# The first two units' inverses: from one pass over 32 rows through DRAM to 16-row blocks joined on TensorE

## The chip, the cores and the metric

The kernel runs on one core of a Trainium2 chip. The metric is the device time of one execution in microseconds (us); lower is better. TensorE is called PE here, VectorE DVE, ScalarE ACT, GpSimd POOL, and SyncE, whose queue issues most DMAs, SP.

## What is computed

A delta-rule attention over 768 tokens for 4 batches of 8 heads of width 48, then an MLP with a squared ReLU on the joined heads. Inputs are float32 (q, k, v, beta) and float64 (the MLP's weights).

```python
k_n = k / (norm(k) + 1e-6)
for t in range(S):                       # S = 768
    y[:, :, t] = q[:, :, t] @ state
    v_old = k_n[:, :, t] @ state
    state = state + beta[:, :, t] * outer(k_n[:, :, t], v[:, :, t] - v_old)
x = y, the 8 heads side by side          # 3072 tokens x 384
out = max(x @ w_in, 0) ** 2 @ w_out      # w_in 384 x 2048, w_out 2048 x 384
```

## The kernel before

**Units.** The work is cut into 12 units of 128 tokens of two batches (6 stretches of time, two pairs of batches). Within a unit the recurrence over a chunk of 64 tokens is put as matrix products: for each chunk and head, the inverse T of a unit triangular 64 x 64 matrix made of k k^T and beta. With T, a chunk's values and keys are transformed (`whole`, L439), and the state is carried through the two chunks (`sequential`, L488). The two pairs of batches have a state each, so units 0 and 1 both start from an empty state and do not depend on each other.

**The inverse.** `static` (L296) transposes k and q on PE, copies them to `kq` with ACT and multiplies k by k and k by q. The diagonal 32 x 32 blocks of k k^T go through DRAM (`blocks`), so that each of up to 128 partitions holds one block (`lt`). `invert` (L386) inverts all blocks on DVE by 31 steps of a product (L413, or L415 with beta as a scalar) and a subtraction (L416). The result goes through DRAM again (`inv`) into `tt` and `t1t`, and `whole` puts the off-diagonal 32 x 32 block together with two small products on PE (L454, L462), a copy (L456) and a negation (L466). For units 0 and 1 one call of `invert` treats both units' blocks, one block a partition, 31 steps of up to 256 elements.

**The MLP.** `moe` (L534) transposes y (L541), splits it in a high and a low half of a reduced float32 format (x_h, x_l), and multiplies it with the weights' high and low halves: nine matmuls a tile of 128 hidden columns (L574), then relu, square and cast on ACT (L581, L582, L584), the low half on DVE (L553) and the products with w_out (L561), for 16 hidden tiles taken two by two.

**The weights.** 28 pieces (12 of w_in, 512 columns wide; 16 of w_out, 384 wide) come as float64 (`fetch`, L122) and are turned into a high and a low half (`split_weights`, L135), in place: the halves take the raw piece's room. For a piece: `least` (L138) takes the absolute value of the upper word on ACT (L142) and clamps it from below on POOL (L143); `words` (L146) is four DVE operations (L150, L153, L156, L157), the last of which reads the lower word; `high` (L161) is a cast on ACT (L163); `low` (L166) adds the rest up in PSUM with two or three matmuls (L170, L171) and copies the low half out with ACT (L172). In the first period the remainder a - high is formed on DVE (`remainder`, L177). `least` is issued three pieces ahead in the beginning and one ahead in the first period.

**Order.** PE, DVE, ACT and SP work through their instructions in the order in which the Python code emits them; generators yield between steps, and the order is written by hand. The prologue (L665 to L710) loads, normalises, forms the products of units 0 and 1, inverts both, and carries unit 0 through its state part, with 18 pieces of the weights taken between. Then come eleven periods (L714). Period u interleaves by fractions of the period (`weave`, L613) the MLP of unit u-1, the state part of unit u, the products of unit u+1, its inversion, and the loads and normalisation of unit u+2; in period 1 also the other 10 pieces of the weights. PE's work is the same in every later period.

Weights are fetched by SP in the order of use: three pieces after the loads of k, three and more between the loads of q, the rest (`fetch(NW)`, L698) ahead of the inversion.

Of the kernel before, what the change touches and what calls it, by code (L numbers as in the profile page):

```python
# [20 lines left out]
def kernel(  # L21
# [74 lines left out]
    ttile = []  # L96
    for i in range(2):
        tt = const.tile([P, NC, H, C], F32, name=f"tt{i}")
        nc.gpsimd.memset(tt[:, :, :, :HB], 0.0)
        ttile.append(tt)  # L100
# [19 lines left out]
    AHEAD = 20  # L120
# [10 lines left out]
    def room(x, n):  # L131
        pool, first, second = rooms[x % 2 if x < AHEAD - 1 else 0]
        return pool.tile([P, PC], I32, name=first)[:, :n], pool.tile([P, PC], I32, name=second)[:, :n]

    def split_weights():  # L135


        def least(x):  # L138

            w1 = raws[x][:, :, 1]  # L140
            a, rest = room(x, w1.shape[1])
            nc.scalar.activation(out=a.bitcast(F32), in_=w1.bitcast(F32), func=AF.Abs)  # L142
            nc.gpsimd.tensor_scalar(out=a.bitcast(F32), in0=a.bitcast(F32), scalar1=LEAST, scalar2=None, op0=ALU.max)  # L143
            return x, a, rest

        def words(x, a, rest):  # L146
            raw = raws[x]
            w1 = raw[:, :, 1]

            nc.vector.tensor_scalar(out=a, in0=a, scalar1=3, scalar2=0x3FFFFFF8,  # L150
# [15 lines left out]
        def low(x, a, rest, hl, formed=False):  # L166
            ps = split_bank()[:, :hl.shape[2]]
            first = [(plus, hl[:, 1])] if formed else [(ident, a.bitcast(F32)), (minus, hl[:, 0])]
            for m, y in first:
                nc.tensor.matmul(ps, lhsT=m, rhs=y, start=(m is first[0][0]), stop=False)  # L170
# [4 lines left out]
        def remainder(x, a, rest, hl):  # L175

            nc.vector.tensor_tensor(out=hl[:, 1], in0=a.bitcast(F32), in1=hl[:, 0].bitcast(F32), op=ALU.subtract)  # L177

        before, ready, x = None, [], 0
        while split_early:  # L180

            far = 3 if x < AHEAD - 3 else 1
            while len(ready) < far:
                ready.append(least(x + len(ready)))
            if x == 0:
                yield
            now = high(*words(*ready.pop(0)))
            if before:
                low(*before)
            before = now  # L190
            x += 1
            while len(ready) < (far if x < AHEAD - 3 else 1):
                ready.append(least(x + len(ready)))
            yield
# [571 lines left out]
```

## Time and profile before

| | |
|---|---|
| median of 3 runs | 695.78 us (695.34 to 696.73) |
| profiled execution: span, first to last instruction | 691.8 us; its own time is not given apart from it, the three runs lie 3.5 to 4.9 us above it |
| PE busy | 628.9 us, 91% of the span |
| DVE busy | 433.1 us, 63% |
| ACT busy | 332.8 us, 48% |
| POOL busy | 76.4 us, 11% |
| mean granted PE clock | 0.966 |
| a later period (transposes of unit 2's MLP at 217.0, of unit 1's at 168.4) | 48.6 us |

The page shows busy times by engine, the span in 40 slices (about 17.3 us each, busy tenths as digits), and groups of instructions: line, engine, operation, written tile <- read tiles, shape, count | busy us, mean ns | idle time of the engine ahead of them and what ended it. A timeline row has the start and the length in us; DMA rows have the time that issuing took.

### The profile page before, as it was taken

The page shows a single profiled execution, that of the slowest core. Times are in us where ns is not written, and L with a number is a line of the kernel's source. Part 1 is how long each engine was busy: PE and PEld are TensorE (multiplying, and loading weights), DVE is VectorE, ACT ScalarE, POOL GpSimd, SP SyncE. Part 2 cuts the span into 40 slices and gives each one's busy share as a digit, 9 for nine tenths or more (in the row PEclk, how much of TensorE's full clock was granted, in tenths as well). Part 3 has the DMA queues.
Part 4 walks back from the last instruction along what each step waited for, and adds up shares of the span by engine and source line. Part 5 has one row for each costly group of instructions (what it writes and reads, how often), then busy time and mean ns, then how long its engine had stood idle before and what let it go on. Part 6 is the DMA issues. An engine that isn't in the chain of part 4 may idle for free.

```text
span 691.8 us, 23593 instructions
## 1 busy us (share of the span) xinstructions
PE 628.9 (91%) x10084; PEld 583.2 (84%) x10084; DVE 433.1 (63%) x1175; ACT 332.8 (48%) x632; POOL 76.4 (11%) x94
## 2 busy tenths in 40 slices
PE   1740797889999999999999999999999999999997
PEld 0530366779999999999999999999999999999997
DVE  3789776898468387477485494694674775641221
ACT  3630455763453544544535535535545445354352
POOL 8540332310100100001001001001000010000000
PEclk9985689999999999999999999999999999999999
DMA  7678620410441531532423414405315324030100
GB/s 158 158 207 290 195 48 5 91 24 2 89 81 20 103 67 23 107 55 39 96 48 55 99 28 77 90 17 114 65 18 107 58 36 97 3 61 3 24 2 23
DMA packets 174712, 49.95 MB, mean 72 GB/s; under 512 B 166400, under 2 KB 169488, under 8 KB 174608
## 3 DMA queue, kind: packets, MB, share of 16 engines
q1 hardware_dynamic: 172016, 47.85, 32.4%
q8 instruction: 79, 1.29, 0.8%
q10 hardware_dynamic: 2336, 0.59, 0.4%
q14 instruction: 25, 0.20, 0.1%
q0 software_dynamic: 256, 0.01, 0.1%
HBM read 37.32 MB, written 11.01 MB: 70 GB/s over the span
## 4 chain that ended last, share of the span: by engine, by line
PE 78%; DVE 4%; ACT 1%; issue 1%; DVEq 0%
PE h L574 30%; PE o L561 29%; PE g L505 3%; PE g L481 3%; PE x L518 2%; PE x L474 2%; PE x L327 2%; PE g L526 1%; PE g L327 1%; PE g L317 1%; PE x L317 1%; PE h L541 1%; PE x L462 1%; PE x L454 1%; DVE tmp L415 1%
## 5 line engine op out<-in xcount | busy, mean ns | idle before, releaser
L561 PE MATMUL o<-w,h_h 128*128 128x384 f32 x768 | 203.7, 346 | 0.0
L574 PE MATMUL h<-x_h,w 128*128 128x256 f32 x1152 | 173.4, 286 | 1.7 <-ACT x_h L543 1.7
L574 PEld LDWEIGHTS h<-x_h,w 128*128 128x128 f32 x1152 | 153.6, 189 | 7.3 <-ACT x_h L543 2.0
L553 DVE TENSOR_TENSOR h_l<-r,h_h 128x512 fp32r<-128x512 f32 x96 | 66.6, 694 | 147.9 <-PE o L561 61.5
L581 ACT ACTIVATE r<-h 128x512 f32<-128x512 f32 x96 | 57.5, 599 | 179.0 <-PE h L574 178.7
L561 PEld LDWEIGHTS o<-w,h_h 128*128 128x128 f32 x768 | 133.2, 188 | 2.4
L561 PE MATMUL o<-w,h_l 128*128 128x384 f32 x384 | 129.8, 338 | 0.0
L415 DVE SCALAR_TENSOR_TENSOR tmp<-lt,bt,z 128x126 f32<-128x126 f32 (+22 forms) x310 | 95.4, 308 | 22.7 <-DMA out_dram<-a 10.5
L574 PE MATMUL h<-x_l,w 128*128 128x256 f32 x576 | 99.8, 282 | 0.0
L416 DVE TENSOR_TENSOR z<-z,tmp 128x126 f32<-128x126 f32 (+22 forms) x310 | 79.2, 255 | 10.7
L574 PEld LDWEIGHTS h<-x_l,w 128*128 128x128 f32 x576 | 82.1, 190 | 0.0
L561 PEld LDWEIGHTS o<-w,h_l 128*128 128x128 f32 x384 | 72.2, 188 | 0.0
L582 ACT ACTIVATE r<-r 128x512 f32<-128x512 f32 x96 | 60.7, 632 | 3.0
L584 ACT CAST h_h<-r 128x512 fp32r<-128x512 f32 x96 | 59.5, 620 | 3.1
L399 POOL MEMSET z<- 128x512 f32 x10 | 5.3, 532 | 401.4 <-DMA inv<-z 355.0
L143 POOL TENSOR_SCALAR a<-a 128x384 f32<-128x384 f32 (+1 forms) x19 | 26.6, 1399 | 47.0 <-ACT a L142 46.8
L274 DVE TENSOR_REDUCE n<-rest 128x8 f32<-128x384 f32 x20 | 10.8, 549 | 31.5 <-ACT rest L273 31.5
L466 ACT ACTIVATE tt<-x 32x256 f32<-32x256 f32 x42 | 15.7, 375 | 26.3 <-PE x L462 25.8
L170 PE MATMUL o<-r,plus 128*128 128x512 f32 (+1 forms) x16 | 10.4, 737 | 19.8 <-DVE r L153 19.8
L543 ACT CAST x_h<-h 128x384 fp32r<-128x384 f32 x24 | 11.6, 482 | 32.2 <-PE h L541 32.2
L505 PEld LDWEIGHTS g<-state,kq 48*64 48x64 f32 x1408 | 22.5, 134 | 4.3 <-issue 2.8
L481 PE MATMUL g<-vt,tt 64*64 64x48 f32 x768 | 25.8, 223 | 0.0
(143 smaller groups left out, 774.2 us busy)
## 6 DMA issues: line engine op xcount, KB each, us to landing
w<-in_moe_w_in_dram SPq DMA_DIRECT2D x12, 512.0 KB
w<-in_moe_w_out_dram SPq DMA_DIRECT2D x16, 384.0 KB
lt<-blocks SPq DMA_DIRECT2D x22, 256.0 KB
vt<-in_v_dram SPq DMA_DIRECT2D x96, 48.0 KB
out_dram<-a SPq DMA_DIRECT2D x46, 96.0 KB
kpad<-in_k_dram SPq DMA_DIRECT2D x88, 48.0 KB
qpad<-in_q_dram SPq DMA_DIRECT2D x88, 48.0 KB
blocks<-ap SPq DMA_DIRECT2D x48, 64.0 KB
```

Of the source, the lines that this page charges most:

```text
L143: nc.gpsimd.tensor_scalar(out=a.bitcast(F32), in0=a.bitcast(F32), scalar1=LEAST, scalar2=None, op0=ALU.max)
L327: nc.tensor.matmul(ps[j][b * C:(b + 1) * C, p], lhsT=kq[rows, c, p, b, 0], rhs=kq[rows, c, p, b, first:first + n].rearrange("p x t -> p (x ...
L415: nc.vector.scalar_tensor_tensor(out=tmp, scalar=bt[:, s:s + 1], op0=ALU.mult, op1=ALU.mult, **factors)
L416: nc.vector.tensor_tensor(out=z[:, :nj, s + 1:], in0=z[:, :nj, s + 1:], in1=tmp, op=ALU.subtract)
L481: nc.tensor.matmul(g[rows, c, h], lhsT=tt[rows, c, h], rhs=vt[rows, c, h], start=True, stop=True)
L505: nc.tensor.matmul(dst[to * C:(to + 1) * C, j, p], lhsT=kq[rows, c, p, b, x], rhs=s[rows, b, p], start=(x == 0 and p == 0), stop=False, sk ...
L553: nc.vector.tensor_tensor(out=h_l, in0=r, in1=h_h.bitcast(F32), op=ALU.subtract)
L561: nc.tensor.matmul(o[i], lhsT=a[:, e, i * P:(i + 1) * P], rhs=halves["wo", ft][w], start=(ft == 0 and n == 0), stop=(ft == FT - 1 and n == 2))
L574: nc.tensor.matmul(hp[:, e], lhsT=halves["wi", (kt, ft // EACH)][w][:, f], rhs=x[:, kt], start=(n == 0), stop=(n == 3 * KT - 1))
L581: nc.scalar.activation(out=r, in_=hp, func=AF.Relu)
L582: nc.scalar.activation(out=r, in_=r, func=AF.Square)
L584: nc.scalar.copy(out=h_h, in_=r)
```

## The change

It touches the prologue, the first period and the weights' conversion. The rest of the periods is as before.

- **Inverses of units 0 and 1.** A new generator `first_pair` takes both units together. It multiplies k by k in 32 x 32 blocks directly on PE, diagonal and off-diagonal ones; turns the diagonal blocks with DVE transposes so that each partition holds rows of 16 x 16 blocks; inverts those on DVE in 15 steps; and joins 16-row blocks to 32 and 32-row blocks to 64 with small matmuls. Nothing of it goes through DRAM. beta comes in 32 small DMAs from POOL's queue in place of 16. Its large temporaries use rooms of weights that are fetched later.
- **State parts.** `whole` is split: what follows the inverse is `applied`. Units 0 and 1 both go through `applied` and `sequential` in the prologue, and the two transposes of unit 0's MLP too; period 1 has no state part.
- **Normalisation.** One call takes k of units 0 and 1 together.
- **Weights.** The clamp moves from POOL to DVE. Absolute value, clamp, the four word operations and the cast stand together in one step, with nothing issued ahead; the low half is always formed by three matmuls. A step of the generator is now a high half or a low half. 22 steps (12 high halves, 10 low ones) are taken in the prologue and 34 in period 1. Pieces 0 to 9 alternate between two pairs of rooms (before 0 to 18).
- **Loads.** k of both units comes ahead of all weights; q, v and 15 weights follow; the loads of unit 2 come next, and the last 13 weights behind them.

The core of the diff; the parts of `first_pair` that shape its blocks are shortened.

```diff
-    AHEAD = 20
+    AHEAD = 10
...
-        def least(x):
-            w1 = raws[x][:, :, 1]
-            a, rest = room(x, w1.shape[1])
-            nc.scalar.activation(out=a.bitcast(F32), in_=w1.bitcast(F32), func=AF.Abs)
-            nc.gpsimd.tensor_scalar(out=a.bitcast(F32), in0=a.bitcast(F32), scalar1=LEAST, scalar2=None, op0=ALU.max)
-            return x, a, rest
-        def words(x, a, rest):
+        def words(x):
             raw = raws[x]
             w1 = raw[:, :, 1]
+            a, rest = room(x, w1.shape[1])
+            nc.scalar.activation(out=a.bitcast(F32), in_=w1.bitcast(F32), func=AF.Abs)
+            nc.vector.tensor_scalar(out=a.bitcast(F32), in0=a.bitcast(F32), scalar1=LEAST, scalar2=None, op0=ALU.max)
...
+        before = None
+        for x in range(NW):
+            now = high(*words(x))
+            yield
             if before:
                 low(*before)
+                yield
             before = now
...
+    def first_pair(ds):
...
+        for r in range(2):
+            for j in range(2):
+                for half in range(2):
+                    for i, d in enumerate(ds):
...
+                        for e in range(2):
+                            nc.gpsimd.dma_start(out=bt[at + e:at + HS:2, j], in_=src[:, :, e * HS:(e + 1) * HS])
...
+        near = blocks(0)
+        yield
+        f = apool.tile([P, 2, HS, 2, HS], F32, name="lt", bufs=1)
+        gs = wide(NW - 7, 2, 2 * NX, HB)
+        for j in range(2):
+            nc.scalar.copy(out=gs[:, j], in_=near[j])
+            nc.vector.transpose(out=f[:, j].rearrange("p t e s -> p (t e s)"),
+                                in_=gs[:, j].rearrange("p i (e t) -> p t (i e)", e=2))
+        yield
+        os = wide(NW - 6, 2, 2 * NX, HB)
+        for j, ps in enumerate(blocks(1)):
+            nc.scalar.copy(out=os[:, j], in_=ps)
+        yield
...
+        for s in range(HS - 1):
+            nj, nt = s + 1, HS - 1 - s
+            tmp = room[:, :2 * nj * nt].rearrange("p (x j t) -> p x j t", x=2, j=nj)
+            nc.vector.tensor_tensor(out=tmp, in0=lt[:, :, s:s + 1, s + 1:].broadcast_to([P, 2, nj, nt]),
+                                    in1=z[:, :, :nj, s:s + 1].broadcast_to([P, 2, nj, nt]), op=ALU.mult)
+            nc.vector.tensor_tensor(out=z[:, :, :nj, s + 1:], in0=z[:, :, :nj, s + 1:], in1=tmp, op=ALU.subtract)
...
+        nc.vector.tensor_tensor(out=all_heads(slice(HS, HB)), in0=all_heads(slice(HS, HB)), in1=ps, op=ALU.subtract)
+        t1 = apool.tile([P, 2 * H2, HB], F32, name="lt", bufs=1)
+        nc.vector.transpose(out=t1, in_=all_heads(slice(0, HB)))
+        nc.scalar.copy(out=all_heads(slice(HB, C)), in_=all_heads(slice(0, HB)))
...
-    NS = 3 * (NW + 1 - (1 + 6 + 4 + 7)) + 2
+    NS = 2 * NW - 22
...
+        ds_.append(load(1))
+        pair = first_pair(ds_[:])
+        take(pair, 1)
+        fetch(3)
         load_q(ds_[0])
         fetch(2)
         load_q(ds_[1])
+        fetch(4)
+        for d in ds_:
+            load_v(d)
+        fetch(6)
+        take(normalize(*ds_))
+        take(pair, 1)
         take(splits, 1)
+        take(pair, 1)
+        take(splits, 1)
+        take(splits, 1)
+        take(splits, 1)
+        take(pair, 2)
+        take(splits, 1)
+        take(pair, 1)
+        take(splits, 1)
+        take(pair, 1)
         ds_.append(load(2))
         load_q(ds_[2])
         load_beta(ds_[2])
+        take(pair, 1)
+        take(splits, 2)
+        take(pair, 1)
+        take(splits, 2)
+        take(pair, 1)
+        take(splits, 1)
+        take(pair, 2)
+        fetch(NW)
+        take(splits, 1)
         third = normalize(ds_[2])
+        for d in ds_[:2]:
+            for _ in applied(d):
+                take(splits, 1)
+        current = moe(ds_[0])
+        for d in ds_[:2]:
+            for _ in sequential(d):
+                take(splits, 1)
+                take(third, 1)
+            if d is ds_[0]:
+                take(current, 2)
+        take(third)
...
-            parts.append((state_part(ds_[u]), 7, *Q1))
+            if u > 1:
+                parts.append((state_part(ds_[u]), 7, *Q1))
```

More of the change, by code (lines that the diff above doesn't have):

```diff
@@ L94 @@
     nc.gpsimd.memset(qp[:, :, :, D:], 0.0)
[L96 to L100, printed above, removed]
+    ttall = const.tile([P, NU, NC, H, C], F32, name="tt")
+    ttile = [ttall[:, i] for i in range(NU)]
+    parity = const.tile([P, 2], F32, name="parity")
+    for e in range(2):
+        nc.vector.tensor_reduce(out=parity[:, e:e + 1], in_=eye.rearrange("p (n e) -> p n e", e=2)[:, :, e], axis=AX.X,
+                                op=ALU.add)
     state = []
@@ L164, in high, with low @@
             return x, a, rest, hl
[L166 removed]
+        def low(x, a, rest, hl):
             ps = split_bank()[:, :hl.shape[2]]
[L168 to L170 removed]
+            nc.tensor.matmul(ps, lhsT=ident, rhs=a.bitcast(F32), start=True, stop=False)
+            nc.tensor.matmul(ps, lhsT=minus, rhs=hl[:, 0], start=False, stop=False)
             nc.tensor.matmul(ps, lhsT=plus, rhs=rest.bitcast(F32R), start=False, stop=True)
@@ L418, in invert @@
         nc.vector.tensor_tensor(out=z, in0=z, in1=bt.unsqueeze(1).broadcast_to([P, J, HB]), op=ALU.mult)
-        invs = [dram.tile([4, H2, HB, HB], F32, name="inv") for _ in range(2 // nz)]
+        inv = dram.tile([4, H2, HB, HB], F32, name="inv")
         for g in range(2):
-            half = z[g * C:(g + 1) * C]
-            nc.sync.dma_start(out=invs[g].rearrange("n h j t -> (n h) j t") if both else
-                              invs[0].rearrange("n h (j g) t -> g (n h) j t", g=2)[g], in_=half)
@@ new lines, in invert @@
+        rows = ttile[d["u"] % 2].rearrange("p c h t -> p (c h) t")
+        for n in range(4):
+            t = slice(n % 2 * HB, (n % 2 + 1) * HB)
+            nc.sync.dma_start(out=rows[n * HB:(n + 1) * HB, :, t], in_=inv[n].rearrange("h s t -> s h t"))
+        d["t1t"] = t1t = apool.tile([P, H, HB], F32, name="t1t", bufs=1)
+        for n in range(4):
+            nc.sync.dma_start(out=t1t[n * HB:(n + 1) * HB],
+                              in_=inv[n // 2 * 2].rearrange("(k j) s t -> j s k t", j=2)[n % 2])
@@ L467, in whole, with applied @@
         yield
+        yield from applied(d)
+    def applied(d):
+        u, kp, vt, kq = (d[x] for x in ("u", "kp", "vt", "kq"))
+        tt = ttile[u % 2]
         ps = [x_tile(u).rearrange("p (c n t) -> p c n t", c=NC, n=NP) for _ in range(2)]
```

302 lines of the change are left out of this document (155 added, 147 removed).

## Prediction

> **What bounds the kernel now.** I read the page first, then a table by stage, then the rows of the transposes that open each period's MLP part, then the groups by line and the timeline of the beginning.
>
> ```profile
> PE   1740797889999999999999999999999999999997
> ...
> DVE  3789776898468387477485494694674775641221
> ...
> PEclk9985689999999999999999999999999999999999
> ```
>
> ```profile
> L541 PE MATMUL h<-plus,y x6: 270/272/273, 105.0 to 107.3; 128*128 128x128 f32 x6
> L541 PE MATMUL h<-plus,y x6: 271/272/273, 168.4 to 170.0; 128*128 128x128 f32 x6
> L541 PE MATMUL h<-plus,y x12: 271/272/273, 217.0 to 267.4; 128*128 128x128 f32 x12
> ```
>
> ```profile
> core 0: us, PE busy (x) PEld busy (x) DVE busy (x) ACT busy (x) POOL busy (x), PEclk, DMA share, GB/s
> 0.00:105.00 105.00, 55.89 (x809) 36.86 (x810) 78.84 (x173) 45.62 (x101) 46.55 (x58) 0.82 0.64 174
> 105.00:168.40 63.40, 54.37 (x783) 49.78 (x782) 51.04 (x125) 37.27 (x73) 12.26 (x9) 0.95 0.17 33
> 168.40:217.00 48.60, 48.60 (x840) 46.41 (x838) 31.67 (x95) 23.70 (x44) 1.96 (x3) 1.00 0.34 65
> ```
>
> From slice 10 on PE never stops (168.4 to 217.0 is one period, 48.60 of 48.60 busy). The change touches nothing after its period 1, so the whole question is when the transposes of unit 1's MLP start: 168.4 us now. Every microsecond by which they move is a microsecond of the span; all later PE work is the same. Before that point lie a prologue of 105 us, in which DVE works 78.8 us and PE 55.9, and a period 1 of 63.4 us instead of 48.6, in which DVE works 51.0. That is DVE's part of the kernel, and what feeds it is ACT.
>
> **What the change removes.** Its largest item is the inversion of the first pair (groups by line, then the timeline; rows picked):
>
> ```profile
> L413 DVE TENSOR_TENSOR h_h<-lt,tt 128x31 f32<-128x31 f32 (+15 forms) x31 | 11.8, 382 | 1.1
> ...
> L416 DVE TENSOR_TENSOR tt<-tt,h_h 128x31 f32<-128x31 f32 (+15 forms) x31 | 11.6, 373 | 1.1
> ...
> L418 DVE TENSOR_TENSOR tt<-tt,bt 128x1024 f32<-128x1024 f32 x1 | 1.2, 1225 | 0.0
> ...
> L447 DVE STREAM_TRANSPOSE t<-t1t 128x256 f32<-128x256 f32 x12 | 5.3, 439 | 2.1 <-DMA t1t<-inv 2.1
> ```
>
> ```profile
> 39.81 0.19 DVE L413 TENSOR_TENSOR h_h<-lt,tt 128x31 f32<-128x31 f32 x1
> ...
> 41.95 0.30 DVE L413 TENSOR_TENSOR h_h<-lt,tt 128x135 f32<-128x135 f32 x1
> ...
> 67.69 1.70 SPq L422 DMA_DIRECT2D inv<-tt  x2
> ...
> 78.68 0.22 PE L454 MATMUL x<-tt,ap 32*32 32x32 f32 x2 [1.74 <-DMA tt<-inv]
> ```
>
> Gone are 62 operations (11.8 + 11.6), the two factors by beta (1.2 each) and the trip through DRAM, 67.69 to 78.68, 11 us. New on DVE: 30 steps on 31 to 135 elements, between 0.19 and 0.30, so 0.25 and a gap of 0.03 each: 8.5; six factors on 512 elements (half of the 1024 row, 0.6), 3.6; eight 512-element transposes by the 256-element row, between 0.44 and twice that, I take 0.85 as they are nearly twice as long: 6.8; a subtraction, 0.7. Sum 19.6 against 25.8 + 0.9: DVE gains 7 us and no trip through DRAM is left.
>
> **What it adds to every weight.** A weight's conversion costs, in means over both widths:
>
> ```profile
> L142 ACT ACTIVATE a<-w 128x384 f32<-128x384 f32 (+1 forms) x19 | 11.6, 609 | 4.9 <-DVE w L177 3.3 <-issue 1.1 <-DMA w<-in_moe_w_out_dram 0.4
> ...
> L150 DVE TENSOR_SCALAR a<-a 128x384 int32<-128x384 int32 (+1 forms) x19 | 8.3, 439 | 2.3 <-POOL a L143 2.3
> ...
> L153 DVE SCALAR_TENSOR_TENSOR a<-w,a 128x384 int32<-128x384 int32 (+1 forms) x19 | 12.3, 650 | 0.7
> ...
> L156 DVE TENSOR_SCALAR w<-a 128x384 int32<-128x384 int32 (+1 forms) x19 | 9.1, 481 | 1.3
> ...
> L157 DVE SCALAR_TENSOR_TENSOR rest<-w 128x384 fp32r<-128x384 uint32 (+1 forms) x19 | 12.0, 633 | 1.4
> ...
> L163 ACT CAST w<-a 128x384 fp32r<-128x384 f32 (+1 forms) x19 | 10.8, 568 | 8.8 <-DVE rest L157 8.8
> ...
> L172 ACT CAST w<-o 128x512 fp32r<-128x512 f32 (+1 forms) x17 | 9.2, 541 | 0.7 <-PE o L171 0.7
> ...
> L177 DVE TENSOR_TENSOR w<-a,w 128x384 fp32r<-128x384 f32 (+1 forms) x10 | 5.9, 593 | 2.6 <-ACT w L163 2.5
> ```
>
> The clamp on DVE is not in the trace; its bounds are L150's 0.44 (one input, a constant, same tile) and L153's 0.65 (two inputs). I take 0.44, the same form of operation. DVE then spends 0.44 + 0.44 + 0.65 + 0.48 + 0.63 = 2.64 us on a weight instead of 2.20; 28 weights add 12 us, and the ten remainders that go (L177) give 5.9 back. DVE's total hardly moves: -7 + 12 - 6 = -1 us.
>
> POOL's clamps, 28 of them, no longer run beside DVE. What a POOL operation does to DVE's first one on a weight:
>
> ```profile
> 27.91 0.36 DVE L150 TENSOR_SCALAR r<-r 128x384 int32<-128x384 int32 x1 [2.27 <-POOL r L143]
> ...
> 30.31 1.38 POOL L373 TENSOR_SCALAR_AFFINE_SELECT ap<-ap 64x512 f32<-64x512 f32 x2
> ...
> 30.38 0.80 DVE L150 TENSOR_SCALAR a<-a 128x384 int32<-128x384 int32 x1 [0.28 <-POOL a L143]
> ```
>
> The same operation takes 0.36 us alone and 0.80 beside POOL. I let that gain stand against the gaps of 0.03 to 0.1 between DVE's operations, which the means leave out. [...]
>
> **The order is what costs.** The engines run in the order of emission. Before, the absolute value is issued up to three weights ahead in the prologue and one ahead in period 1, so ACT does it while DVE is at an earlier weight. In the new code it stands directly ahead of the weight's own five DVE operations, and the cast stands directly behind them; the cast writes over the raw words, so it waits for L157:
>
> ```profile
> 124.83 0.70 DVE L157 SCALAR_TENSOR_TENSOR rest<-w 128x512 fp32r<-128x512 uint32 x1
> ...
> 125.56 0.62 ACT L163 CAST w<-a 128x512 fp32r<-128x512 f32 x1 [0.19 <-DVE rest L157]
> ```
>
> ```profile
> L581 ACT ACTIVATE r<-h 128x512 f32<-128x512 f32 x96 | 57.5, 599 | 179.0 <-PE h L574 178.7
> ...
> L582 ACT ACTIVATE r<-r 128x512 f32<-128x512 f32 x96 | 60.7, 632 | 3.0
> L584 ACT CAST h_h<-r 128x512 fp32r<-128x512 f32 x96 | 59.5, 620 | 3.1
> ...
> L318 ACT COPY kq<-x 128x512 f32<-128x512 f32 x24 | 13.1, 590 | 0.6 <-PE x L317 0.6
> ```
>
> Between the two ACT stands still for 2.64 us at every weight, and everything queued behind the cast (relu, square and cast of the MLP, the copies out of PSUM for which PE waits, the next absolute value) waits with it. DVE in turn has only as much other work as stands between two weights. A weight's round: 0.61 + 2.64 + 0.57 + the low half's copy 0.54 + 0.08 for four hand-overs (125.53 to 125.56 is one of 0.03) = 4.4 us.
>
> *Period 1.* The prologue now takes 22 steps of a generator with two steps a weight, that is twelve weights; sixteen are left where ten were. Sixteen rounds: 16 x 4.4 = 70.4. Ahead of the last one stand seven of the MLP's triples (0.60 + 0.63 + 0.62 = 1.85), 13.0; four kq copies, 2.4; the third normalisation's three, estimated 1.2. Sum 87 us from the first absolute value to the last cast. Both ways: ACT's neighbours overlap by about 0.1 us, which takes 6 off; DVE's inversion steps of unit 2 and waits on PE can put 8 on. Behind the last cast come its three matmuls and some four MLP steps on PE, 5 us, to the transposes of unit 1. What goes from period 1, unit 1's state part, is PE and DVE work that lay beside this; with 16 rounds on ACT it brings nothing.
>
> *Prologue.* Times at which each stage's last ACT or DVE operation ends, in the order of emission, from the rows above and three more:
>
> ```profile
> 7.12 0.94 ACT L273 ACTIVATE rest<-kpad 128x384 f32<-128x384 f32 x2 [3.66 <-DMA kpad<-in_k_dram]
> ```
>
> ```profile
> L286 DVE TENSOR_TENSOR kpad<-kpad,s 128x768 f32<-128x768 f32 x12 | 11.6, 964 | 0.3 <-DMA kpad<-in_k_dram 0.2
> ...
> L256 POOL DMA_DIRECT2D bt<-in_beta_dram x8 | 4.5, 590 | 0.0
> ```
>
> k of unit 0 is there at 7.1; that of unit 1, now with no weight ahead of it, I put at 10.3; squares, sums, roots and two factors of 0.96 end at 15.7, transposes and copies at 19. Three weights and a low half: 32. Nine copies (diagonal and off-diagonal blocks, low half, q): 37.5. Weight 3: 41. Levels to 16 on DVE, 15.6 of the 19.6: 57; beneath it lie the products' copies, a low half and an absolute value. Weights 4 and 5 with ys and a low half: 64. Subtraction, copy of all heads (twice 0.6), low half, four copies of m, four negations: 71.5. Weight 6: 75. Both applied parts, six copies and weight 7: 84. Both sequential parts: four weights with four low halves, 17.5, and copies of y and x_h, sums of the state and the third normalisation, estimated 6.5: 108. Ends: 100 if ACT's overlaps count fully, 114 if PE's slower clock shows in each of the ten small stages.
>
> Behind other work and counted at nothing: 32 beta transfers on POOL, 32 x 0.59 = 19 us, over by 24 where beta is needed at 41; if they took twice that, they would be late by 2. On SP the loads of unit 2 wait for unit 1's q transposes (37) with the last thirteen weights behind them; weight 15 is needed at some 123, so 50 us or more cover them; each microsecond beyond would count in full.
>
> *Sum.* 108 + 87 + 5 = 200 against 168.4: +31.6. Span 691.8 + 31.6 = 723.4, and with the 4.0 between this span and the median of 695.78: **727 us**. The ends 100 + 81 + 5 and 114 + 95 + 5 give 713 and 741.
>
> **Rivals.** *DVE alone sets period 1* (the idle ACT costs nothing, as DVE has other steps to do). DVE's 51.0 less 5.9 of remainders and about 4 of state part plus 16 x 2.64 - 10 x 2.20 = 61.3, and some 4 of gaps between some 130 operations: 65. 108 + 65 + 5 = 178, 705 us. For it: the share of 51.0 in 63.4 now. Against: unit 2's inversion, DVE's main other work, is emitted only from 0.4 of the period.
>
> *Faster.* The prologue ends by 90, as the DRAM trip (11) and the 7 us of DVE suggest, and period 1 takes DVE's 65: 160, 687 us. It decides once prologue and period 1 together fall below 168.4 - 5 = 163; with a prologue of 108 a round would have to take (55 - 16.6) / 16 = 2.4 us, and its DVE operations alone take 2.64.
>
> *A cold PE, slower still.* In period 1 PE has some 46 us of work in 87: today's 54.4, less about 12 for unit 1's state part, plus about 4 for the matmuls of the further weights, both estimated.
>
> ```profile
> 113.00:114.00 1.00, 0.00 (x0) 1.00 0.00 0
> ...
> 117.00:118.00 1.00, 1.00 (x7) 0.50 0.00 0
> ```
>
> (A stretch, its length, PE's busy time, its clock.) Here some 2 us of idling, the stretch before 114 among them, were followed by a clock of 0.50 at 117. In period 1 of the new code PE idles about as long in each round. If the low clock held for all of it, 46 would become 92, more than the chain: period 1 some 97, 737 us. [...]
>
> **Chances.** Forecast (711 to 734) 0.60; cold PE or more waits (734 to 747) 0.18; DVE alone (702 to 711) 0.11; faster 0.08; no change 0.03. A difference within 0.2% (1.4 us) is about what a measurement here can't tell. The range 705 to 743 leaves out the faster cases (0.08), no change (0.03), and about a third of the cold case and of the third (0.10 together). Faster 0.08, same 0.03, slower 0.89.
>
> **What would show it.** Right: in period 1 ACT's cast waits for the weight's last DVE operation at each of sixteen weights, 2 us or more each, casts some 5 us apart; the transposes for unit 1's MLP near 200 us; the period after it 48.6 us again; before that both units' state sums near 85 to 108. Wrong: casts under 4 us apart, DVE over 90% busy in period 1, or a prologue that ends before 95.

## The result and the profile after

| | before | after |
|---|---|---|
| median of 4 runs beside each other | 696.25 us (695.34 to 699.17) | 746.05 us (741.95 to 747.47) |
| ratio | | 1.0713 [1.0666, 1.076] |
| profiled execution: time, span | span 691.8 us | 744.84 us, span 743.1 us |
| PE, DVE, ACT, POOL busy | 628.9, 433.1, 332.8, 76.4 us | 660.0, 429.0, 335.2, 48.1 us |
| mean granted PE clock | 0.966 | 0.931 |

The change makes the kernel 50 us slower. The prediction had 727 us (705 to 743): the side was right, the size short by 19 us and the range missed by 3. The page of the kernel after, busy tenths in 40 slices of 18.6 us:

```profile
PE   2626876787689999999999999999999999999997
...
DVE  3585146447774675764937748558476494661211
...
PEclk9775578788699999999999999999999999999999
```

PE is full from the thirteenth slice (223 us) on. That puts the whole loss into the first 220 us, which the transposes of the MLP show (units 1 and 2, six each):

```profile
L632 PE MATMUL h<-plus,y x6: 271/272/272, 220.1 to 221.7; 128*128 128x128 f32 x6
```

```profile
L632 PE MATMUL h<-plus,y x6: 270/272/273, 269.6 to 271.2; 128*128 128x128 f32 x6
```

Unit 1's transposes start at 220.1 instead of 168.4, 51.7 us later; behind them lie 743.1 - 220.1 = 523.0 us, before 691.8 - 168.4 = 523.4. In every experiment below this rest is 522 to 525 us, so the start of unit 1's transposes (called T1) tells all. One of e4's four runs below took 1061.73 us at a granted clock of 0.559, the other three 740.53 to 740.71, and its ratio goes by those three.

The prologue's last weight is the twelfth: its absolute value stands at 124.08 and its cast ends at 127.54. Period 1's sixteen weights begin with the absolute value at 127.82:

```profile
124.08 0.55 ACT L145 ACTIVATE a<-w 128x384 f32<-128x384 f32 x1
127.03 0.51 ACT L160 CAST w<-a 128x384 fp32r<-128x384 f32 x1 [2.40 <-DVE rest L154]
...
127.82 0.55 ACT L145 ACTIVATE a<-w 128x384 f32<-128x384 f32 x1
```

By stage, cut at the twelfth weight's absolute value, so that the second row holds seventeen casts:

```profile
core 0: us, PE busy (x) PEld busy (x) DVE busy (x) ACT busy (x) POOL busy (x), PEclk, DMA share, GB/s
0.00:124.00 124.00, 71.08 (x2129) 56.58 (x2129) 63.10 (x136) 42.88 (x82) 30.56 (x58) 0.71 0.48 130
124.00:220.00 96.00, 71.22 (x380) 58.23 (x379) 62.09 (x151) 42.53 (x84) 0.00 (x0) 0.84 0.12 22
```

No engine is full in either stretch. DVE's total before T1 is 125 us, before 78.84 + 51.04 = 130: DVE does have less to do, and nothing came of it. What fills the second stretch is a wait (waits of 124 to 220: us, times, longest), one at each of the seventeen casts:

```profile
ACT w L160 <- DVE rest L154: 48.4, 17, 3.9
DVE a L146 <- ACT a L145: 20.9, 12, 7.4
```

ACT's 42.53 us of work and 48.4 us of standing at the cast are 91 of the 96 us. Two of the casts (start, length, line, what was waited for and how long):

```profile
172.50 0.51 ACT L160 CAST w<-a 128x384 fp32r<-128x384 f32 x1 [2.41 <-DVE rest L154]
...
182.47 0.62 ACT L160 CAST w<-a 128x512 fp32r<-128x512 f32 x1 [2.87 <-DVE rest L154]
```

Here the weight's absolute value is what stands ahead of the cast on ACT, and 2.4 to 2.9 us is DVE's five operations. By this view it is the order of ACT's queue that costs, not ACT's load. In the groups by line, ACT's idle time ahead of the 28 casts was 17.3 us before (L163, 8.8 and 8.5 in its two groups) and is 94.7 now (L160, 80.7 and 14.0); the larger of the two groups is shown, and the clamp on DVE, which takes 385 ns:

```profile
L160 ACT CAST w<-a 128x384 fp32r<-128x384 f32 (+1 forms) x23 | 12.7, 553 | 80.7 <-DVE rest L154 80.7
...
L146 DVE TENSOR_SCALAR a<-a 128x384 f32<-128x384 f32 (+1 forms) x23 | 8.8, 385 | 39.2 <-ACT a L145 39.2
```

### The profile page after: what moved, and what is told of

Read it like the earlier page. It is cut to its first block, busy times and chain, and to the rows that moved or that the text cites. A ratio compares the mean times of both kernels' runs of the same rounds, so it can differ in the third digit from the quotient of the medians.

```text
span 743.1 us, 25321 instructions
## 1 busy us (share of the span) xinstructions
PE 660.0 (89%) x11000; PEld 610.3 (82%) x11000; DVE 429.0 (58%) x1168; ACT 335.2 (45%) x623; POOL 48.1 (6%) x85
## 3 DMA queue, kind: packets, MB, share of 16 engines
q8 instruction: 86, 1.41, 0.8%
## 4 chain that ended last, share of the span: by engine, by line
PE 80%; DVE 11%; ACT 4%; issue 3%; DMA 1%; SPq 0%; DVEq 0%; ACTq 0%
PE h L665 28%; PE o L652 27%; PE g L572 3%; PE g L596 3%; PE x L565 2%; PE x L609 2%; PE g L617 2%; PE o L165 1%; DVE a L150 1%; PE x L295 1%; DVE rest L154 1%; PE g L295 1%; DVE w L153 1%; PE g L285 1%; PE x L285 1%
## 5 line engine op out<-in xcount | busy, mean ns | idle before, releaser
L665 PE MATMUL h<-x_h,w 128*128 128x256 f32 x1152 | 177.5, 291 | 4.0 <-ACT w L168 3.1
L665 PEld LDWEIGHTS h<-x_h,w 128*128 128x128 f32 x1152 | 158.2, 194 | 10.0 <-ACT w L168 3.4
L665 PEld LDWEIGHTS h<-x_l,w 128*128 128x128 f32 x576 | 83.9, 194 | 0.0
L160 ACT CAST w<-a 128x384 fp32r<-128x384 f32 (+1 forms) x23 | 12.7, 553 | 80.7 <-DVE rest L154 80.7
L596 PEld LDWEIGHTS g<-state,kq 48*64 48x64 f32 x1408 | 24.3, 142 | 9.1 <-ACT a L145 4.5
L596 PE MATMUL g<-state,kq 48*64 48x48 f32 x1408 | 27.0, 228 | 5.1 <-ACT a L145 4.4
L146 DVE TENSOR_SCALAR a<-a 128x384 f32<-128x384 f32 (+1 forms) x23 | 8.8, 385 | 39.2 <-ACT a L145 39.2
L165 PE MATMUL x<-a,plus 128*128 128x384 f32 (+1 forms) x36 | 18.4, 597 | 13.3 <-DVE a L150 9.7
```

The costliest lines, as they stand in the source:

```text
L165: nc.tensor.matmul(ps, lhsT=ident, rhs=a.bitcast(F32), start=True, stop=False)
L596: nc.tensor.matmul(dst[to * C:(to + 1) * C, j, p], lhsT=kq[rows, c, p, b, x], rhs=s[rows, b, p], start=(x == 0 and p == 0), stop=False, sk ...
L665: nc.tensor.matmul(hp[:, e], lhsT=halves["wi", (kt, ft // EACH)][w][:, f], rhs=x[:, kt], start=(n == 0), stop=(n == 3 * KT - 1))
```

## The experiments

Theory A: the order of a weight's conversion on two in-order engines costs most of the 50 us, and more weights are left for period 1. Theory B: something that the prediction counted at nothing (DVE's load, POOL, a cold PE, transfers) costs it. All times are medians; T1 is from the transposes' rows. Before had T1 at 168.4, after at 220.1.

| run | us | before beside it | ratio | T1 |
|---|---|---|---|---|
| e1_abs_ahead | 722.25 | 694.35 | 1.0407 [1.0347, 1.0468] | 195.2 |
| e2_clamp_pool | 770.03 | 694.35 | 1.1103 [1.1028, 1.1178] | 243.5 |
| e8_abs_twice | 752.30 | 694.35 | 1.0837 [1.0774, 1.0901] | 228.2 |
| e4_before_tight | 740.63 | 694.35 | 1.0676 [1.0604, 1.0747] | 214.8 |
| e3_before_clamp_dve | 715.36 | 696.08 | 1.029 [1.0221, 1.0359] | 190.4 |
| e12_clamp_in_words | 698.68 | 694.45 | 1.0071 [1.004, 1.0102] | 169.8 |
| e7_pair_old_split | 723.57 | 696.08 | 1.0399 [1.0338, 1.0461] | 196.0 |
| e9_state1_back | 741.36 | 694.45 | 1.0697 [1.0626, 1.0768] | 215.2 |
| e14_pair_only | 709.78 | 693.69 | 1.0218 [1.0187, 1.0249] | 185.6 |
| e5_no_mask | 740.85 | 696.08 | 1.0655 [1.0587, 1.0723] | 213.1 |
| e6_warm_pe | 762.64 | 696.08 | 1.0971 [1.0911, 1.1032] | 237.8 |
| e10_warm_fit | 744.56 | 694.45 | 1.0735 [1.0675, 1.0795] | 222.6 |
| e13_fetch_later | 738.72 | 693.69 | 1.0645 [1.0618, 1.0672] | 214.2 |

**Is it the order? e1: after, with the absolute value a step ahead and the cast a step behind.** The work is the same; only the places on ACT move. Left out of the cut are `least`, split off from `words`, and one half step more in the prologue.

```diff
-        before = None
+        before, ready = None, least(0)
         for x in range(NW):
-            now = high(*words(x))
+            now = words(*ready)
             yield
             if before:
                 low(*before)
+            before = high(*now)
+            if x + 1 < NW:
+                ready = least(x + 1)
+            if x < NW - 1:
                 yield
-            before = now
```

> The changed kernel, with each weight's absolute value issued a step ahead (before the next weight's DVE operations) and its cast a step later, together with the low half of the weight before; clamp still on DVE, as many weights in period 1. Theory 'order' (ACT stands still between absolute value and cast, so a round of ACT and DVE in a row sets the pace): period 1, 96 us from the first absolute value to unit 1's transposes in the changed kernel, falls to DVE's own 65 to 72, the prologue gains 6 to 10: 746 becomes 705 to 722. Rival 'load' (the clamp on DVE and six more weights in period 1 make DVE the bound): no more than 5 us gained, 740 or more. Rival 'cold PE' (the small stages at half clock cost the time): 735 or more, with PE's clock as low as now.

24 us come back (746 to 722), about the least that was expected of the order (705 to 722). This kernel from its twelfth weight's cast (114.34) to T1, and the wait at the casts there:

```profile
114.00:195.00 81.00, 64.53 (x367) 50.35 (x366) 59.88 (x147) 42.15 (x81) 0.00 (x0) 0.92 0.14 25
```

```profile
ACT w L164 <- DVE rest L158: 27.2, 15, 4.4
```

The sixteen casts of period 1 are 4.63 us apart (117.79 to 187.30) where they were 5.60 (130.84 to 214.91), and the wait at the cast falls from 48.4 to 27.2 us, over seventeen casts in both. About half of the 24 us comes ahead of that: the twelfth weight's cast starts 12.7 us earlier. From that cast to T1 it takes 81 us, not the 65 to 72 that were expected if DVE set the pace: DVE is busy in 59.88 of them.

**Or the load? e2: after, with the clamp given to POOL again. e8: after, with the absolute value done twice.** e2 takes the clamp's 0.385 us off DVE and leaves the order, with a third engine in the row; e8 makes the row longer by one ACT operation.

```diff
-            nc.vector.tensor_scalar(out=a.bitcast(F32), in0=a.bitcast(F32), scalar1=LEAST, scalar2=None, op0=ALU.max)
+            nc.gpsimd.tensor_scalar(out=a.bitcast(F32), in0=a.bitcast(F32), scalar1=LEAST, scalar2=None, op0=ALU.max)
```

> The changed kernel with only the clamp put back on POOL, everything else in the new order. 'Order': the clamp stands in the round, where POOL takes 1.40 us instead of DVE's 0.39, so 28 rounds get 1.0 us longer each: 765 to 778. 'Load': DVE has 11 us less to do, 730 to 742. 'Cold PE': no change within 5 us.

```diff
             nc.scalar.activation(out=a.bitcast(F32), in_=w1.bitcast(F32), func=AF.Abs)
+            nc.scalar.activation(out=a.bitcast(F32), in_=a.bitcast(F32), func=AF.Abs)
```

> The changed kernel with the absolute value taken twice (the second of the first, so the values stay the same): one more ACT operation of 0.61 us in each round and no more DVE work. 'Order': 28 x 0.55 to 0.61, so 14 to 18 us more, 758 to 764. 'Load': nothing, as ACT is busy for 45% of the span, 744 to 749. 'Cold PE': 744 to 752.

DVE with less to do is 24 us slower in e2: a load theory has the wrong sign. The waits of e2 from 130 to 245 show each link of the row:

```profile
ACT w L160 <- DVE rest L154: 65.3, 18, 4.1
DVE a L147 <- POOL a L146: 39.0, 17, 7.1
```

In e8 the casts of period 1 are 6.03 us apart, 0.43 more, which is what a second operation of 0.55 us behind the first costs when neighbours on ACT overlap by 0.1 (in the kernel after L168 takes 0.47 us from 127.45, and the next row starts at 127.82); T1 moves by 8.1. The total of 6 us is below the 14 to 18 that were expected and at the upper edge of what was expected of a cold PE, since the prologue ended only 1.2 us later: its stage between the casts of weights 6 and 7 (counted from 0) took 9.4 us instead of 12.5, which e10 below comes back to.

**Does it need the rest of the change? e4, e3, e12: before, with the conversion alone.** e4 puts the whole new conversion (order, clamp, low half by three matmuls) into the kernel before, where 18 weights stay in the prologue. e3 moves only the clamp to DVE, where it was issued, up to three weights ahead. e12 moves it to the head of the weight's own words; the absolute value stays ahead.

```diff
-        def least(x):
...
+            nc.scalar.activation(out=a.bitcast(F32), in_=w1.bitcast(F32), func=AF.Abs)
+            nc.vector.tensor_scalar(out=a.bitcast(F32), in0=a.bitcast(F32), scalar1=LEAST, scalar2=None, op0=ALU.max)
             nc.vector.tensor_scalar(out=a, in0=a, scalar1=3, scalar2=0x3FFFFFF8,
...
+        before = None
+        for x in range(NW):
+            now = high(*words(x))
+            yield
             if before:
                 low(*before)
+                yield
             before = now
...
-    NS = 3 * (NW + 1 - (1 + 6 + 4 + 7)) + 2
+    NS = 2 * NW - 36
```

> The kernel before (inversion of the pair through DRAM, unit 1's state part in period 1) with the new conversion of the weights and nothing else: absolute value, clamp on DVE, word operations and cast in a row, low half by three matmuls, 36 half steps in the prologue. 'Order': each round costs some 1 to 2 us that nothing covers, on 28 weights: 715 to 740. 'Load': DVE has 11 us more to do and 6 less without the remainders: 698 to 704. If the on-chip inverse is what costs: 695 to 700.

```diff
             nc.scalar.activation(out=a.bitcast(F32), in_=w1.bitcast(F32), func=AF.Abs)
-            nc.gpsimd.tensor_scalar(out=a.bitcast(F32), in0=a.bitcast(F32), scalar1=LEAST, scalar2=None, op0=ALU.max)
+            nc.vector.tensor_scalar(out=a.bitcast(F32), in0=a.bitcast(F32), scalar1=LEAST, scalar2=None, op0=ALU.max)
             return x, a, rest
```

> The kernel before with only the clamp moved from POOL to DVE; absolute values stay up to three weights ahead. 'Order': 11 us more on DVE, of which gaps in the beginning take a part and which POOL's absence pays back in part: 693 to 704. 'Load': 11 us of DVE work come out at the end in full, 706 or more.

```diff
             nc.scalar.activation(out=a.bitcast(F32), in_=w1.bitcast(F32), func=AF.Abs)
-            nc.gpsimd.tensor_scalar(out=a.bitcast(F32), in0=a.bitcast(F32), scalar1=LEAST, scalar2=None, op0=ALU.max)
             return x, a, rest
         def words(x, a, rest):
...
+            nc.vector.tensor_scalar(out=a.bitcast(F32), in0=a.bitcast(F32), scalar1=LEAST, scalar2=None, op0=ALU.max)
```

> The kernel before with the clamp on DVE, but at the head of the word operations instead of right behind the absolute value: the absolute value stays ahead, the clamp does not. The same DVE work as in the kernel before with the clamp moved as it stands (715 us). If that one lost by DVE standing at each clamp for an absolute value queued behind a cast (1.5 us at each weight in its timeline): 690 to 702 here. If it lost by the clamp's DVE time: 710 or more.

e4 is slower by 46 us: the new conversion (order, clamp and low half together), with nothing else of the change, costs almost as much as the whole change. Unit 0's transposes start at 135.9 instead of 105.0, and period 1 takes 78.9 us instead of 63.4.

e3 was a miss of mine: 19 us slower where the order was to cost at most 8, and 706 us or more had been put down to DVE's load. By its time alone it speaks for the load; its rows show another cause, which e12 then tests. DVE now meets the clamp three weights before it needs it, and the absolute value behind which it waits is queued behind a cast on ACT:

```profile
30.17 0.36 DVE L143 TENSOR_SCALAR a<-a 128x384 f32<-128x384 f32 x1 [1.61 <-ACT a L142]
```

The clamp itself takes 0.36 us, the wait ahead of it 1.61. Up to 129 us, where unit 0's transposes start (before 105.0), these waits come to 31 us (e3, waits of 0 to 129):

```profile
DVE r L143 <- ACT r L142: 19.7, 8, 5.1
...
DVE a L143 <- ACT a L142: 11.4, 7, 2.0
```

e12 does the same DVE work as e3, its clamps wait 0.6 us in all up to 135, and it is 4 us slower than the kernel before beside it (0.7%, 0.4 to 1.0) where e3 is 19: with its operand ready, the clamp on DVE costs little. Some 15 of the 19 us are where it stands, not its time.

**What do the pair's inverse and the state parts cost? e7, e9, e14.** e7 is the kernel after with the old conversion (clamp on POOL, absolute values ahead, remainder on DVE in period 1), twelve weights in the prologue. e9 is the kernel after with unit 1's sequential part in period 1 again. e14 is the kernel before with the pair's inverse on chip, and with the loads and the joint normalisation of the change, but nothing else of it: old conversion, 18 weights in the prologue, unit 1's state part in period 1.

```diff
+        before, ready, x = None, [], 0
+        while split_early:
+            far = 3 if x < AHEAD - 3 else 1
+            while len(ready) < far:
+                ready.append(least(x + len(ready)))
...
+            now = high(*words(*ready.pop(0)))
...
-    NS = 2 * NW - 22
+    NS = 3 * (NW - 12) + 2
```

> The changed kernel's first pair on chip, both state parts ahead, loads as in the changed kernel, but the weights' conversion of the kernel before (absolute value and clamp three ahead, clamp on POOL, remainder on DVE in period 1), again twelve weights in the prologue. 'Order': the prologue ends near 110 instead of 124, period 1 takes 73 to 78: 708 to 724. 'Load': as DVE has no clamp, 700 to 735, and no waiting of ACT for the weight's last DVE operation is needed for that. If the on-chip inverse with both states ahead pays in itself: below 696.

```diff
-        for d in ds_[:2]:
-            for _ in sequential(d):
-                take(splits, 1)
-                take(third, 1)
-            if d is ds_[0]:
-                take(current, 2)
+        for _ in sequential(ds_[0]):
+            take(splits, 1)
+            take(third, 1)
+        take(current, 2)
+        take(splits, 4)
         take(third)
...
+            else:
+                parts.append((sequential(ds_[u]), 4, *Q1))
```

> The changed kernel with unit 1's sequential part back in period 1 (unit 1's applied part and the pair's inverse stay in the prologue, and as many weights are converted there). 'Order': the sequential part's PE and DVE work lies beside ACT's standing in period 1, the prologue loses the stages between its four last steps: 4 to 8 us less, 738 to 742. If having both states ahead helps, as period 1 has less on PE: 748 to 756.

```diff
-        pair = [static(d) for d in ds_[:2]]
...
+        pair = first_pair(ds_[:])
...
-        take(invert(ds_[0]))
...
-        for _ in state_part(ds_[0]):
+        for _ in state_tail(ds_[0]):
             take(splits, 1)
...
-            parts.append((state_part(ds_[u]), 7, *Q1))
+            parts.append((state_part(ds_[u]), 7, *Q1) if u > 1 else (state_tail(ds_[u]), 5, *Q1))
```

`state_tail` is `applied` and then `sequential`.

> The first pair's inverse on chip alone: loads and first_pair as in the changed kernel, but the weights' conversion of the kernel before, 18 weights in the prologue, and unit 1's applied and sequential parts in period 1. If the on-chip inverse saves DVE's 7 us and the 11 us through DRAM: 680 to 692. If PE's pauses and its low clock in the joins eat that up: 693 to 706. If first_pair is what costs most of the 50 us: 715 or more.

e7 is still 27 us slower than before: with the good conversion, the rest of the change loses too. Its time lies in the ranges of both theories, so it doesn't choose between them. Against it, the new conversion costs 22 us, as e1 says from the other side (24). e9 shows no gain from carrying unit 1's sequential part ahead: without it T1 is 4.9 us earlier, and the time 3 us nearer to before's. That it costs something isn't shown, as the intervals of the two ratios overlap and 3.1 of the 4.9 us had come by weight 7's cast, ahead of the edit. e14 is 16 us slower, between the ranges I had set. Its prologue (unit 0's transposes at 119.1, before 105.0) has what the inverse saved and where that went; first e14, then before, from 62 to 90:

```profile
62.00:90.00 28.00, 21.86 (x785) 16.45 (x783) 11.10 (x19) 12.37 (x23) 9.19 (x7) 0.62 0.41 136
```

```profile
62.00:90.00 28.00, 17.65 (x234) 10.05 (x236) 23.08 (x53) 11.88 (x26) 8.38 (x7) 0.62 0.73 233
```

DVE is busy for 11.10 us there instead of 23.08: it stands, since the joins hand each result from PE to ACT or DVE and back (waits of e14, 60 to 120):

```profile
DVE n L275 <- ACT r L274: 9.7, 1, 9.7
DVE tt L533 <- PE h L531: 8.1, 1, 8.1
```

Before, the 11 us of the trip through DRAM were filled with weights. In e14 nothing is free to fill the joins: ACT's queue holds the joins' copies, which wait for PE, and the squares of the third normalisation behind them.

**POOL's mask. e5: after, without the four affine selects of units 0 and 1**, so q k^T isn't masked there and the results of these units differ.

```diff
-            for b in range(2):
-                half = d["ap"][b * C:(b + 1) * C, :, :, 1].rearrange("p c h t -> p (c h) t")
-                nc.gpsimd.affine_select(out=half, in_=half, pattern=[[0, H2], [1, C]], base=0, channel_multiplier=-1,
-                                        compare_op=ALU.is_gt, fill=0.0)
```

> The changed kernel without POOL's four affine selects on the first pair's k q products (units 0 and 1 are left unmasked, so those units' outputs are not the reference's). In the changed kernel's timeline six of the 38 small DVE operations between 43 and 49 us take 1.0 to 1.3 us instead of 0.2 to 0.3 while POOL runs these. If POOL holds DVE up: the inversion's stage ends 4 to 5 us earlier and the whole run is 4 to 5 us shorter, 740 to 742. If the overlap costs nothing on the path: 744 to 747.

First the kernel after, POOL and the inversion's small DVE operations; then e5:

```profile
43.24 5.08 POOL L454 TENSOR_SCALAR_AFFINE_SELECT ap<-ap 64x1024 f32<-64x1024 f32 x4 [17.82 <-ACT ap L451]
```

```profile
44.87 1.01 DVE L471 TENSOR_TENSOR z<-z,tmp 128x30 f32<-128x30 f32 x1
...
55.64 0.21 DVE L471 TENSOR_TENSOR z<-z,tmp 128x30 f32<-128x30 f32 x1
```

```profile
43.68 0.19 DVE L467 TENSOR_TENSOR z<-z,tmp 128x30 f32<-128x30 f32 x1
```

The same operation takes 1.01 us beside POOL and 0.21 or 0.19 without. The cast of weight 4, right behind the inversion, comes at 60.08 instead of 63.83, 3.75 us earlier. T1 comes 7.0 us earlier and the run is 5 us nearer to before's. What goes beyond 3.75 came between the casts of weights 6 and 7 (9.3 us instead of 12.5); runs that keep the mask have that too, so it isn't the mask's.

**A cold PE? e6 and e10: after, with idle 128 x 128 matmuls in four gaps of the pair's stages** (140, 25, 20, 20 and 65, 8, 6, 6).

```diff
+        warm_up(65)
         take(pair, 1)
         take(splits, 2)
+        warm_up(8)
         take(pair, 1)
...
+    def warm_up(n):
+        g = ps_g.tile([P, 2, PC], F32, name="g")
+        for _ in range(n):
+            nc.tensor.matmul(g[:, 0, :P], lhsT=ident, rhs=ident, start=True, stop=True)
```

> The changed kernel with idle matmuls between the first pair's stages (140 ahead of the products that join 16-row blocks, 25, 20 and 20 between the next), so that PE's clock stays up. If the cold PE is what made the prologue 16 us longer than forecast: the stretch from the 16-row products to the end of the joins, 62 to 86 us now, gets 5 to 9 us shorter, 737 to 741. If ACT and DVE in a row set it: within 2 us of 746.

> The idle matmuls once more, fewer: in the first try each took 0.21 us of PE at full clock instead of 0.11, and 140 of them held the next stage up by 12 us. Now 65, 8, 6 and 6, so that they end before the stage behind them is due. 'Cold PE' (half clock from 46 to 95 us in the changed kernel made the joins 7 to 10 us longer than forecast): the stretch from weight 4's cast at 64 to weight 6's at 89 gets 5 to 9 us shorter, 737 to 742. If only ACT and DVE in a row set it: 744 to 748.

e6's time tells nothing: the first 140 idle matmuls lasted until 73.8 us and held up the products behind them, which end at 77.0 instead of 64.9. In e10 the first ones were done at 55.9, the clock was 0.82 to 0.86 from 70 to 85 where it is 0.50 in the kernel after, and the time stayed (744.56). From weight 5's cast to weight 6's it even took 22.9 us instead of 18.2, with a pause of 3.47 us on PE among the last idle matmuls. But a single group of the joins shows what the clock does to it; first the kernel after, then e10:

```profile
75.29 1.92 PE L509 MATMUL h<-tt,w 32*32 32x32 f32 x64
```

```profile
77.21 1.20 PE L510 MATMUL h<-tt,w 32*32 32x32 f32 x64
```

The same 64 matmuls take 0.7 us less (1.20 in e6 too), at a clock of 0.82 in e10 from 75 to 80 and of 0.50 in the kernel after, and ACT's copy behind them starts as much earlier. The applied parts say the same: from weight 6's cast to weight 7's the kernel after took 12.5 us at a mean clock of 0.76; e2, e5, e6, e8, e9, e10 and e13, which change little or nothing in that stage, took 8.7 to 10.5 us. In e10 the clock is 0.62 from 90 to 95 and 1.00 from 95 to 100, where the kernel after has 0.53 and 1.00, and the stage takes 10.2 us from 93.2 on; in e13 it is 0.81 from 84 to 88, and the stage takes 8.7 us from 86.6 on. So a cold PE goes with some 2 to 4 us there. No run sets the clock and leaves the rest, so what it costs in the joins as a whole stays open.

**The last weights' transfers. e13: after, with the last 13 fetches held until unit 1's applied part is done**, by a small transfer on SP that reads its result.

```diff
-        fetch(NW)
         take(splits, 1)
...
+        gate = dram.tile([P, 4], F32, name="gate")
+        nc.sync.dma_start(out=gate, in_=ds_[1]["vt"][:, 0, 0, :4])
+        fetch(NW)
         current = moe(ds_[0])
```

> The changed kernel with the last 13 weights' fetches held back until unit 1's values have been transformed (some 98 us) by a small transfer ahead of them on SP's queue that reads those values. In the changed kernel PE pauses inside groups of like small matmuls, with nothing shown that it waits for: 3.9 and 2.6 us in the 32 x 32 products at 22 to 32 us, 1.4, 2.2, 2.2 and 0.7 in the joins at 63 to 86. If the weights' transfers hold up PE's instructions: the pauses of the joins (2.2 and 2.2) go below 0.7, the joins get 3 to 5 us shorter, 738 to 743. If the rate at which instructions come in sets the pauses: they stay, and the time too, 743 to 749; weights that then come late would add to that.

T1 comes 5.9 us earlier. In the kernel after, ACT's rows of the joins show where the transfers had struck (DMA share 0.96 from 75 to 80, in e13 0.01 from 76 to 80), then e13:

```profile
77.25 1.18 ACT L512 COPY w<-h 32x512 f32<-32x512 f32 x2 [1.38 <-PE h L509]
78.96 1.18 ACT L512 COPY w<-x 32x512 f32<-32x512 f32 x2 [0.53 <-PE x L509]
82.91 1.20 ACT L521 ACTIVATE tt<-x 32x512 f32<-32x512 f32 x2 [2.78 <-PE x L519]
```

```profile
80.73 1.20 ACT L521 ACTIVATE tt<-x 32x512 f32<-32x512 f32 x2 [0.41 <-PE x L519]
```

The first negation waits 0.41 us for PE instead of 2.78. From weight 5's cast to weight 6's it takes 15.0 us instead of 18.2 (17.6 to 19.0 in e2, e5, e8 and e9, which hold no fetch back), so some 3 us in the joins are the transfers'. From there to weight 7's it takes 8.7 instead of 12.5, but those four runs have 9.3 to 10.5 there as well, so most of this part can't be put down to the transfers.

So neither theory has it all. The conversion is about half of the 50 us (22 by e7, 24 by e1), and the rest of the change is the other half (27 by e7), in which the pair with its loads (16 by e14), POOL's mask (3.75) and, in the joins, the transfers (some 3) have their parts. No version here beats the kernel before; the nearest is e12.

## Why the prediction came out short

- **Only T1 matters, and the rest stays.** Right: 523.0 us behind it, before 523.4.
- **The conversion's order.** Right: e1 gets 24 us back with the same work, and e2 and e8, which lengthen the row, lose. In the old kernel the whole new conversion costs 46 us (e4); the clamp's own time is some 4 there (e12). That 46 and 24 differ fits the new prologue's other waits, in which part of it can hide; no run takes that apart.
- **The chain of period 1.** Forecast 87 us (81 to 95), measured 87.6 from the first absolute value (127.8) to the end of the last cast (215.4), and 4.7 instead of 5 from there to T1. Its inner picture held: a wait of 2.4 us or more at every cast, casts 5.6 us apart (some 5 forecast).
- **DVE's total hardly moves.** Right: -5 us before T1 (-1 forecast). The clamp was 0.385 us, taken as 0.44.
- **The prologue: this term failed.** "Ends: 100 if ACT's overlaps count fully, 114 if PE's slower clock shows in each of the ten small stages": it ended at 127.5, with the twelfth weight's cast, against 108. These 19.5 us are the whole miss. By stage, forecast and measured ends: nine copies 37.5 and 38.8; weight 3 41 and 42.2; levels to 16 57 and 61.5; weights 4 and 5 64 and 71.05; joins 71.5 and 85.8; weight 6 75 and 89.2; applied parts and weight 7 84 and 101.85; sequential parts with four weights 108 and 127.5. So up to weight 3 the sum was right within 1.3 us, and the rest of the miss came in five steps:
  - 3.3 us in the levels to 16. I had counted beta's transfers as POOL's work and let POOL's mask stand beside DVE at no cost. e5 shows 3.75 us. The prediction had quoted the row that says so (0.80 instead of 0.36 beside POOL) and used it for the clamps alone. In the kernel after, four small operations (six in e5's expectation) take 1.01 to 1.18 us beside the selects. They end at 44.61, 45.88, 47.20 and 48.41, and the four selects at 44.56, 45.84, 47.13 and 48.32, each within 0.1 us ahead of one of them.
  - 7.3 us in the joins. I summed DVE's and ACT's operations and left out PE's groups between them, though each hands over to the next: ACT waits 1.38, 0.53, 2.78 us there in the rows above. These groups ran at a clock of 0.50, where 64 matmuls take 1.92 us instead of 1.20. In two of them PE pauses for 2.2 us each with nothing that the profile shows it to wait for; in e13 one pause is gone and the other shorter.
  - 3.6 us in the applied parts with weight 7. In seven other runs the stage is 2 to 4 us shorter (in e10 with a clock of 1.00 from 95 on), which would leave little of this miss; the profiled run had 0.76.
  - 2.6 us at weights 4 and 5, where one of PE's pauses (1.38 us) stands; not taken apart by any run.
  - 1.7 us in the sequential parts with their four weights, not taken apart either.
- **Transfers.** I asked only whether the last weights come in time (they do), not what they take from the stages that they run beside. T1 is 5.9 us earlier in e13; some 3 us, in the joins, go with them.
- **The rivals.** DVE alone (705): refuted, DVE was busy in 62.09 of 96 us. Faster: refuted; the prologue ended at 127.5, and e14 shows that the inverse on chip, even with the old conversion, is a loss of 16 us here. A cold PE in period 1: PE's clock was 0.84 in it, not 0.50, and its chain was ACT's and DVE's.

What stays open: why the pair costs 16 us by itself in parts (its waits are shown, no run removed them one at a time); what makes the other 11 of the 27 us of e7, which also carries unit 1's state part ahead and converts six weights fewer in the prologue; and what a warm PE would give in the joins.

## What to carry to other kernels

Where two in-order engines hand a piece of work to and fro, count the places in their queues before the durations: here the clamps waited 0.6 us in all where they stood at the head of their own weight's words (e12) and 31 us where they stood right behind the absolute value (e3), and ACT stood for 48.4 us at seventeen casts emitted right behind the operations that they wait for. When a stage is replaced by a chain of small steps over three engines, sum the chain link by link with PE's groups in it, and ask what else can fill the gaps; here the 11 us through DRAM, with DVE busy for 23.08 of 28 us around them, cost less than the joins, with 11.10 of 28. Ask of a moved transfer also what runs beside it, not only whether it lands in time. Before a few microseconds between two profiles are put down to an edit, look whether they came where the edit is: here one stage ahead of several edits differed by 2 to 4 us.

## What the runs showed of the hardware

**PE's pauses, counted in its matmuls and weight loads.** The new groups of 64 to 256 small matmuls are broken by pauses of 0.7 to 3.9 us whose releaser the profile gives as "issue": in the kernel after they end at 22.28, 32.21, 63.52, 71.68, 81.74 and 86.26. The stretches between those ends (PE's and its weight loads' counts in the brackets):

```profile
22.20:32.00 9.80, 5.94 (x256) 3.92 (x256) 6.24 (x11) 3.51 (x7) 3.14 (x6) 0.72 0.80 227
32.10:63.40 31.30, 12.08 (x379) 9.35 (x378) 24.11 (x53) 7.55 (x15) 6.86 (x7) 0.66 0.54 130
63.40:71.60 8.20, 5.94 (x255) 4.76 (x256) 2.60 (x6) 2.53 (x5) 0.00 (x0) 0.50 0.23 70
71.60:81.70 10.10, 7.90 (x255) 6.69 (x255) 1.93 (x2) 3.82 (x6) 1.89 (x2) 0.50 0.72 241
81.70:86.20 4.50, 3.83 (x127) 3.57 (x127) 0.00 (x0) 2.77 (x5) 0.00 (x0) 0.50 0.53 193
```

Taken with a few records missing (379 for 384 at most), these are 256, 384, 256, 256 and 128 matmuls, each with its load: multiples of 256 instructions. In e10, whose idle matmuls put more instructions between, the pauses moved with respect to the code (the fifth from L519 to the idle matmuls ahead of its place), and the distances, taken in the same way (507 for 512 at most), are multiples of 256 instructions again:

```profile
32.50:63.10 30.60, 25.90 (x507) 23.44 (x506) 23.69 (x53) 7.47 (x15) 6.86 (x7) 0.89 0.51 129
63.10:71.90 8.80, 8.27 (x255) 7.41 (x256) 2.75 (x6) 2.53 (x5) 0.00 (x0) 0.61 0.23 65
71.90:83.20 11.30, 7.82 (x256) 6.98 (x256) 1.93 (x2) 3.83 (x6) 1.89 (x2) 0.85 0.78 272
```

So in these two runs the pauses go with the count of PE's instructions, not with the code at the place. The pages' tables of queues have these instruction rows, first the kernel after, then before:

```profile
q8 instruction: 86, 1.41, 0.8%
```

```profile
q8 instruction: 79, 1.29, 0.8%
```

That is 1.41 MB / 86 = 16.4 KB a packet. PE has 22,000 matmuls and loads after and 20,168 before (10,084 of each), which divided by the packets is 256 and 255; which engine's instructions a packet holds, and when it came, the tables do not say.

The six pauses are 13 us (2.59, 3.93, 1.38, 2.21, 2.16 and 0.69). With the weights' transfers held back (e13) the pause in L519 goes (1.9 to 2.7 us in e5, e8 and e9) and that in L496 falls from 2.2 to 1.4 (1.5 to 2.5 there), while those in L416, which stand beside other transfers, stay (3.0 and 4.0). So does the one in L488 (1.4, in e13 1.6), beside which little is moved in either run (7 GB/s in the kernel after, 17 in e13's slice from 55.3 to 73.7). That PE is held up by the weights' transfers can be no more than a part of it; what the pauses wait for no row shows.

**A PE that is busy for 12 us and stays cold.** In e13 the groups of matmuls on 16 to 64 rows, with a weight's low half between, run without a gap (stretch, PE busy, clock):

```profile
72.00:76.00 4.00, 4.00 (x116) 0.50 0.02 4
76.00:80.00 4.00, 4.00 (x165) 0.50 0.01 4
80.00:84.00 4.00, 4.00 (x152) 0.50 0.03 8
```

12.00 us busy of 12, and the clock stays at 0.50; from 84 to 88, with PE busy for 4.00 of 4 us again, it is 0.81. Under the idle matmuls of e10, 128 x 128, it is 1.00 from 45 to 55, with 10.00 us busy of 10. What sets the clock beside how busy PE is, no run shows.
